# Outer-product recurrence and gated feed-forward on one core: another order of loads, v copies, units and split blocks

## The chip, the cores and the metric

The kernel runs on 1 core of one Trainium2 chip. The metric is the device time of one execution in microseconds (us), the median of 3 runs. Its engines are PE (matmuls, with PEld for the weight loads), DVE, ACT and POOL (elementwise work), and SP, which here only issues DMAs. POOL also issues the loads of the weights.

## What is computed

```python
f = 1.0 / (1.0 + np.exp(-f_logit))
for t in range(S):
    state = f[:, :, t, :, None] * state + np.einsum('bhd,bhe->bhde', k[:, :, t], v[:, :, t])
    y[:, :, t] = np.einsum('bhd,bhde->bhe', q[:, :, t], state)
...
x = np.ascontiguousarray(attn_out.transpose(0, 2, 1, 3)).reshape(B * S, H * D)
gate = np.maximum(x @ w_gate, 0.0)
val = x @ w_val
return (gate * val @ w_out).astype(np.float32)
```

There are 4 batches, 8 heads, 768 tokens and 48 columns a head, so x has 3072 rows of 384; the hidden width is 1536.

## The kernel before

**Units.** The recurrence is computed in chunks of 128 tokens. Two neighbouring chunks of a batch make a unit of 256 tokens; there are 12 units, in the order of batches 0 to 3 and then on along the sequence, so units 0 to 3 begin the four batches. A unit loads f, k, q and v (384 KB each, one DMA each, `load`, L465). ACT takes exp and log of f (L535, L542 or L537) to get the negative log of the decay. PE sums it along the chunk with triangular matrices (`cum`, L549 to L551). ACT takes the exponentials of the sums (L564 to L574). DVE and POOL multiply q and k by them; the products are called hats (L586 for units 0 to 3, L592 for the others). Units 0 to 3 turn the hats with PE (L624) and copy them out of PSUM (L401/402, the keys tq and tk of a unit); the later units turn them by a DMA on SP (L635). PE multiplies the turned hats to scores (L649), which are masked with `seen` (L663 on DVE, or L658 on ACT and L660 on POOL). The copies of v into a padded tile (`vpad`, four for a unit, keys v00 to v11) and, in units 0 to 3, of its rest (`vrest`, r0 and r1) are lines L399 (DVE), L401 (ACT) and L402 (POOL). PE builds from hats and v the new state (L704 or L714); DVE and POOL add it up and scale it (L510, L514, L517) with a decay that PE sums (L686, L690) and ACT exponentiates (L695), or, in units with the key td, that a small DMA fetches. PE forms the output of each chunk from masked scores, v and old state (L747, or L754 and L758), and a copy or a DMA brings it transposed into `xT`.

**Groups.** Two units make a group of 512 tokens for the feed-forward, so there are 6 groups. A group has 12 blocks of 128 hidden columns. For each block PE computes gate and value (L798, three matmuls of 512 columns each), ACT takes the relu of the gate (L803) and DVE the product into `gT` (L810). Then PE multiplies `gT` with `wo` (L828, 36 matmuls of 384 columns for every pair of chunks, in steps of three), ACT or DVE copies the result (L401/402) and SP stores it. `PARTS` says which blocks of a group are split: `(0, 2, 0, 3)` is chunks 0 and 1 of blocks 0 to 2, that is the first unit's half, with matmuls of 256 columns; before, only blocks 0 to 2 of group 0 are.

**Weights.** wg, wv and wo come in four slices of three blocks each, issued by POOL (L479), 12 DMAs. `FIRST` lists the first loads, and behind an @ which load a weight slice must wait for.

**Order.** Nothing is scheduled on the chip by rules: each operation has a number, and `SEQUENCE` lists for every engine, and for SP, the numbers in the order of issue. `HOMES` says which results follow each other in each of the 8 PSUM banks. `UNITS` names, for every unit, the engine of each movable step (the keys above, and x0, x1, o0, o1, q and k hats, masks m00 to m11, sum). Engines work strictly in the listed order and wait on semaphores for what they need. `FILLERS` puts warm-up matmuls on zeros (L879, 512 columns) ahead of the waits of some of the first PE steps: 38 in all. Operations that cross the two halves of the partitions on POOL wait for the one before.

The loads on SP begin f0, f1, q1, k0, k1, q0, v2, f2, v0, v1, k2, q2, f3, v3, k3, q3. On ACT the logs of units 0 and 1 come first. POOL has, among others, three copies of v0 and one of its rest, four of v1, one k hat of unit 0, three q hats, and between these the first weight issues. In the first 150 numbers unit 1 is ahead of unit 0 on PE, DVE and ACT for most steps: its hats are turned, its scores formed and its first output made sooner.

Of the kernel before, what the change touches and what calls it, by code (L numbers as in the profile page):

```python
# [5 lines left out]
AF = mybir.ActivationFunctionType  # L6
# [32 lines left out]
class Plan:  # L39
# [91 lines left out]
    def needs(self):  # L131
# [144 lines left out]
PARTS = {0: [(0, 2, 0, 3), (2, 4, 0, 3), (0, 4, 3, 12)]}  # L276
# [5 lines left out]
def bass_hgrn2_outer__then__ffn_reglu_kernel(  # L282
# [10 lines left out]
    B, H, S, D = q.shape  # L293
    C = 128
# [77 lines left out]
    def act_t(n):  # L372
        return dict(occ=0.8 if n == 768 else 0.06 + n / 1200.0, lat=0.16)
# [572 lines left out]
```

## Time and profile before

| | |
|---|---|
| median of 3 runs | 190.05 us (189.39 to 190.53) |
| the profiled execution | 190.12 us |
| its span, from first to last instruction | 188.9 us |
| granted TensorE clock, mean | 1.000 |
| POOL, busy | 103.1 us (55%) |
| DMA | 32.89 MB, mean 174 GB/s |

The profile shows one execution. In its timeline and chain the first number is the start, the second the length in us; "x3" is a count, and what stands in brackets is the idle time of the engine just before, and what ended it. In the groups by line the two numbers behind the bar are busy us in total and the mean ns of one. Matmuls overlap, so their lengths in the timeline are longer than the distance from one to the next; the chain shows the distances. A few matmul records are missing.

### The profile page before, as it was taken

To read this page: it belongs to the slowest core of one execution; us is meant where nothing else is said; L and a number is where in the kernel's file an instruction comes from. 1 tells how busy PE (TensorE), PEld (TensorE's weight loads), DVE (VectorE), ACT (ScalarE), POOL (GpSimd) and SP (SyncE) were. 2 spreads that over 40 slices of the span, in tenths; PEclk is the share of its full clock that TensorE was granted. 3 is DMA by queue.
4 is the path that set the end of the run, shared out by engine and by line. 5 is a ranking of instruction groups with operands and counts; after the bars stand their busy time and mean duration, and the time that the engine had idled before them with its cause. 6 is when DMAs were issued, how large, how long until landed. Compare 5 with 4: busy or idle time off the path is not lost.

```text
span 188.9 us, 4186 instructions
## 1 busy us (share of the span) xinstructions
PE 180.7 (96%) x1626; PEld 99.6 (53%) x1649; DVE 123.8 (66%) x227; ACT 120.5 (64%) x231; POOL 103.1 (55%) x138
## 2 busy tenths in 40 slices
PE   7899999999999999989999999999999999999995
PEld 2355584556654555534655445556555555444564
DVE  4169957778389898956687688996636653454320
ACT  3888869876789888966785776484284422334213
POOL 3299946998097795997744998732839100000000
PEclk9999999999999999999999999999999999999999
DMA  6999999998399999989999969878550240200025
GB/s 161 325 325 280 242 217 204 261 207 130 79 322 227 206 283 245 206 201 212 228 182 305 244 111 162 193 177 203 97 140 14 72 126 3 83 0 0 0 93 202
DMA packets 83167, 32.89 MB, mean 174 GB/s; under 512 B 75334, under 2 KB 83148, under 8 KB 83148
## 3 DMA queue, kind: packets, MB, share of 16 engines
q1 hardware_dynamic: 78348, 29.09, 65.3%
q0 software_dynamic: 4800, 3.54, 12.1%
q8 instruction: 13, 0.21, 0.4%
q14 instruction: 6, 0.05, 0.1%
HBM read 25.96 MB, written 4.73 MB: 162 GB/s over the span
## 4 chain that ended last, share of the span: by engine, by line
PE 82%; POOL 5%; DMA 4%; ACT 3%; issue 3%; DVE 2%; POOLq 0%
PE ps L798 48%; PE ps L828 23%; PE ps L649 3%; PE ps L747 2%; DMA f_in<-in_f_logit_dram 2%; DMA xT<-xn 2%; POOL vpad L402 2%; DVE gT L810 1%; PE ps L758 1%; PE ps L704 1%; POOL hats L586 1%; PE ps L624 1%; ACT bneg L542 1%; DVE hats L592 1%; POOL wg L479 1%
## 5 line engine op out<-in xcount | busy, mean ns | idle before, releaser
L810 DVE TENSOR_TENSOR gT<-relu,ps 128x512 bf16<-128x512 bf16 (+1 forms) x75 | 49.2, 682 | 22.5 <-PE ps L798 12.8
L803 ACT ACTIVATE relu<-ps 128x512 bf16<-128x512 f32 (+1 forms) x75 | 42.2, 579 | 31.3 <-PE ps L798 24.1
L798 PE MATMUL ps<-xT,wg 128*128 128x512 bf16 (+1 forms) x211 | 52.3, 370 | 1.4 <-issue 0.5
L798 PE MATMUL ps<-xT,wv 128*128 128x512 bf16 (+1 forms) x218 | 53.0, 370 | 0.6 <-issue 0.3
L828 PE MATMUL ps<-wo,gT 128*128 128x384 bf16 (+2 forms) x300 | 52.2, 320 | 0.0
L828 PEld LDWEIGHTS ps<-wo,gT 128*128 128x128 bf16 x300 | 28.1, 98 | 19.2
L592 POOL TENSOR_TENSOR hats<-q_in,expo 64x384 bf16<-64x384 f32 x28 | 27.8, 993 | 17.0 <-DMA q_in<-in_q_dram 9.8
L798 PEld LDWEIGHTS ps<-xT,wg 128*128 128x128 bf16 x225 | 21.0, 98 | 21.8 <-DMA xT<-xn 0.5
L798 PEld LDWEIGHTS ps<-xT,wv 128*128 128x128 bf16 x225 | 20.8, 98 | 20.8 <-ACT relu L803 0.3
L660 POOL TENSOR_TENSOR ptm<-ptm,seen 128x512 bf16<-128x512 bf16 x21 | 24.0, 1156 | 3.7 <-ACT ptm L658 3.5
L592 DVE TENSOR_TENSOR hats<-k_in,ps 64x384 bf16<-64x384 f32 x32 | 17.6, 551 | 4.5 <-ACT ps L574 4.0
L663 DVE TENSOR_TENSOR ptm<-ps,seen 128x512 bf16<-128x512 f32 x27 | 17.9, 683 | 2.9 <-PE ps L649 2.8
L517 POOL TENSOR_TENSOR st<-ssum,dec 128x384 bf16<-128x384 f32 x16 | 13.2, 828 | 5.3 <-DMA dec<-rates 3.5
L401 ACT ACTIVATE osb<-ps 128x384 f32<-128x384 f32 (+2 forms) x18 | 8.5, 470 | 10.6 <-PE ps L828 10.3
L658 ACT ACTIVATE ptm<-ps 128x512 bf16<-128x512 f32 x21 | 11.9, 597 | 5.2 <-PE ps L649 5.2
L567 ACT ACTIVATE expo<-ps 128x384 f32<-128x384 f32 x22 | 10.5, 487 | 6.9 <-DVE ps L556 6.2
L402 POOL CAST vpad<-v_in 64x384 bf16<-64x384 f32 x24 | 12.0, 501 | 1.3
L535 ACT ACTIVATE f_in<-f_in 128x768 f32<-128x768 f32 x12 | 10.1, 839 | 2.3 <-DMA f_in<-in_f_logit_dram 2.2
L514 DVE TENSOR_TENSOR ssum<-ps,st 128x384 f32<-128x384 f32 x16 | 8.8, 552 | 3.7 <-PE ps L704 3.1
L879 PE MATMUL ps<-zeros 128*128 128x512 bf16 x36 | 10.7, 434 | 0.2 <-issue 0.2
L574 ACT ACTIVATE ps<-ps 128x384 f32<-128x384 f32 x22 | 10.7, 490 | 0.0
L539 POOL TENSOR_TENSOR bneg<-f_in 128x384 bf16<-128x384 f32 x5 | 5.0, 1001 | 9.5 <-ACT f_in L537 9.5
(89 smaller groups left out, 175.4 us busy)
## 6 DMA issues: line engine op xcount, KB each, us to landing
f_in<-in_f_logit_dram SPq DMA_DIRECT2D x12, 384.0 KB, 5.6
q_in<-in_q_dram SPq DMA_DIRECT2D x12, 384.0 KB, 5.0
k_in<-in_k_dram SPq DMA_DIRECT2D x12, 384.0 KB, 4.8
v_in<-in_v_dram SPq DMA_DIRECT2D x12, 384.0 KB, 4.8
out_dram<-osb SPq DMA_DIRECT2D x22, 192.0 KB, 2.1
wg<-in_moe_w_gate_dram POOLq DMA_DIRECT2D x4, 288.0 KB, 7.8
wv<-in_moe_w_val_dram POOLq DMA_DIRECT2D x4, 288.0 KB, 7.9
wo<-in_moe_w_out_dram POOLq DMA_DIRECT2D x4, 288.0 KB, 8.2
```

Source lines behind the costliest of these rows:

```text
L402: return engine[e].tensor_copy(out, src)
L517: add(e, lambda: engine[e].tensor_tensor(t4(s_new), t4(tmp), rate, ALU.mult), [key] + dk, [f"S{b}_{y}"], **(dict(occ=0.79, lat=0.1) if e = ...
L574: add("ACT", lambda i=i, ex=ex: sc.activation(bc[i].ap[:, 0:HD] if in_place else ex[:, 1, :], bc[i].ap[:, 0:HD], AF.Exp, scale=1.0), [bc[i ...
L592: op = add(e, lambda i=i, n=n, x=x, e=e, y=y, lo=lo, exps=exps: engine[e].tensor_tensor(hats[64 * i:64 * i + 64, hi, y, x, :, 0:D], by_i[n ...
L658: add("ACT", lambda pt=pt, s=sj[j]: sc.activation(pt, s.ap[:, :].rearrange("p (n t) -> p n t", n=NP), AF.Copy), [sj[j]], [f"raw{mis[y]}_{j ...
L660: add("POOL", lambda pt=pt, mask=mask: gp.tensor_tensor(pt, pt, mask, ALU.mult), [f"raw{mis[y]}_{j}", "seen"], [f"raw{mis[y]}_{j}", f"ptm{ ...
L663: add("DVE", lambda pt=pt, mask=mask, s=sj[j]: ve.tensor_tensor(pt, s.ap[:, :].rearrange("p (n t) -> p n t", n=NP), mask, ALU.mult), [sj[j ...
L798: mm = te.matmul(bank.ap[:, 0:n], wt[:, kt, j * 128:(j + 1) * 128], xT[xi][:, kt, n0:n1], start=(kt == 0), stop=(kt == NK - 1))
L803: add("ACT", lambda: sc.activation(relu[ri][:, n0:n1], gate.ap[:, 0:n], AF.Relu), [gate], rk, **act_t(n))
L810: return ve.tensor_tensor(o, a, b, ALU.mult)
L828: mm = te.matmul(bank.ap[:, 0:cut[1] - cut[0]], gT[gi][:, j, r * C:(r + 1) * C], wo[:, j, cut[0]:cut[1]], start=(j == 0), stop=(j == NJ - 1))
L879: return te.matmul(bank[:, 0:WARM], zeros[:, 0:128], zeros[:, 0:WARM], start=True, stop=True, skip_group_check=True)
```

## The change

- SP: the loads begin v0, f0, f1, q0, k1, k0, q1, v1, f2, q2, k2, f3, v2, k3, q3, v3.
- ACT begins with three copies of v0 (v00, v11, v10, which were POOL's); the exponentials and logs of f come behind them, in the order exp f0, exp f1, log f0, log f1. Unit 0's other copies of v and its rest go to DVE (v01, r1) and POOL (r0). Of unit 1, v01, v00 and v11 are on ACT.
- Unit 0 is ahead of unit 1 in hats, scores, masks and state. On POOL the first hats are unit 0's q0, then unit 1's q1 and q0; unit 0's k hats are both on DVE.
- POOL issues wg0 behind unit 1's q1 hat, wg1 behind its q0 hat, wv0 when q2 has landed, wv1 two copies later, wg2 to wg3 behind unit 1's state, wv3 behind a mask of unit 2, and wo0 to wo2 behind unit 3's copies of v3, wo3 behind one more mask.
- Ahead of the feed-forward's first matmul PE has the same steps as before, but for unit 2's decay sum and unit 1's second output, which stand behind it.
- Blocks 0 to 5 of groups 0 and 1 are computed in halves. In group 1 some of the first unit's halves stand ahead of the first L828 of group 0.
- The 38 warm-up matmuls become 30, 18 of them ahead of the first cumulative sum.
- `SEQUENCE`, `HOMES` and the engines in `UNITS` are others for all units. The sum of the two halves of the logs is POOL's in units 3 to 11; before, DVE had it in units 4, 9, 10 and 11. In unit 6, POOL makes the unit's four q hats one after the other; before, one of unit 7 stood ahead of the fourth. The load of q for unit 6 is the fourth behind unit 5's transposes on SP; it was the fifth.
- `load` can take half the heads, and `unit` can take exp and log in two parts (key fs); no unit sets it and no load is halved.

```diff
-FILLERS = {67: (9, 0), 106: (4, 0), 83: (6, 1), 121: (3, 1), 125: (4, 3), 90: (7, 2), 134: (4, 1), 138: (1, 0)}
+FILLERS = {67: (18, 0), 85: (3, 0), 83: (1, 4), 90: (1, 6), 123: (2, 6), 87: (2, 0), 125: (3, 0)}
...
     "ACT": [
-        65, 66, 103, 69, 104, 73, 107, 108, 74, 111, 112, 70, 84, 10, 230, 231, 130, 116, 246, 81, 117, 94, 133, 136, 245, 234, 235, 238, 239,
+        77, 82, 80, 65, 103, 66, 104, 70, 69, 74, 133, 73, 107, 111, 112, 116, 94, 115, 108, 10, 242, 243, 122, 120, 100, 130, 97, 246, 247, 136,
...
     "SP": [
-        37, 41, 43, 38, 42, 39, 48, 45, 40, 44, 46, 47, 49, 52, 50, 51, 142, 271, 143, 311, 144, 274, 145, 272, 273, 317, 388, 389, 320, 435,
+        40, 37, 41, 39, 42, 38, 43, 44, 45, 47, 46, 49, 48, 50, 51, 52, 283, 142, 143, 323, 145, 144, 284, 285, 286, 329, 424, 425, 445, 471,
...
-FIRST = 'f0 k0 q0 v0 f1 k1 q1 v1 f2 k2 q2 v2 f3 k3 q3 v3 wg0@v2 wv0@f0 wg1@v2 wv1 wg2@v2 wv2@f3 wg3@q2 wv3@f0 wo0@f0 wo1@f3 wo2 wo3@f3'
-PARTS = {0: [(0, 2, 0, 3), (2, 4, 0, 3), (0, 4, 3, 12)]}
+FIRST = 'f0 k0 q0 v0 f1 k1 q1 v1 f2 k2 q2 v2 f3 k3 q3 v3 wg0@q0 wv0@q2 wg1 wv1 wg2@v0 wv2 wg3@k0 wv3@q1 wo0@v1 wo1@q0 wo2@k1 wo3'
+PARTS = {0: [(0, 2, 0, 6), (2, 4, 0, 6), (0, 4, 6, 12)], 1: [(0, 2, 0, 6), (2, 4, 0, 6), (0, 4, 6, 12)]}
```

The numbers of the first steps are the same in both kernels: 65 and 66 are exp and log of f0, 103 and 104 of f1; 77, 80 and 82 the copies v00, v10 and v11 of unit 0; 116 the copy v01 of unit 1; 94 and 133 the decays of units 0 and 1; 108 unit 1's k exponential; 37 to 52 the loads f0, k0, q0, v0, f1 and so on. From about 230 on the numbers are shifted, as the split blocks add operations.

More of the change, by code (lines that the diff above doesn't have):

```diff
@@ L534, in unit @@
         on.update(UNITS.get(u, {}))
-        add("ACT", lambda: sc.activation(raw["f"], raw["f"], AF.Exp, scale=-1.0), [f"f{li}"], [f"f{li}"], **act_t(2 * HD))
-        if on["sum"]:
+        fs = on.get("fs")
+        if fs:
+            for x in range(2):
+                part, hs = raw["f"][:, x * HD:(x + 1) * HD], slice(x * NP, (x + 1) * NP)
+                add("ACT", lambda part=part: sc.activation(part, part, AF.Exp, scale=-1.0), [f"f{li}x{x}", f"f{li}"], [f"f{li}x{x}"], **act_t(HD))
+                add("ACT", lambda hs=hs: sc.activation(bn[:, :, hs, 0:D], by_i["f"][:, :, hs, :], AF.Ln, bias=1.0),
+                    [f"f{li}x{x}", f"f{li}", f"bneg{bi}"], [f"bn{bi}x{x}"], **act_t(HD))
+        else:
+            add("ACT", lambda: sc.activation(raw["f"], raw["f"], AF.Exp, scale=-1.0), [f"f{li}"], [f"f{li}"], **act_t(2 * HD))
+        if fs:
+            pass
+        elif on["sum"]:
             add("ACT", lambda: sc.activation(raw["f"], raw["f"], AF.Ln, bias=1.0), [f"f{li}"], [f"f{li}"], **act_t(2 * HD))
@@ L543, in unit @@
                 [f"bn{bi}"], **act_t(2 * HD))
-        bkeys = [f"bneg{bi}", f"bn{bi}"]
+        bkeys = [f"bneg{bi}", f"bn{bi}"] + ([f"bn{bi}x{x}" for x in range(2)] if fs else [])
         bc = [Bank("bc"), Bank("bc")]
```

67 lines of the change are left out of this document (33 added, 34 removed), and 83 rows, old and new, of tables (SEQUENCE, UNITS).

## Prediction

> **What bounds the kernel now.** I read the page's first two parts, then the chain that ended last, then the timeline of the first 27 us with the waits inside it.
>
> ```profile
> PE 180.7 (96%) x1626; PEld 99.6 (53%) x1649; DVE 123.8 (66%) x227; ACT 120.5 (64%) x231; POOL 103.1 (55%) x138
> PE   7899999999999999989999999999999999999995
> PEclk9999999999999999999999999999999999999999
> ```
>
> TensorE is busy in every slice at full clock, so from the first feed-forward matmul on, its own work sets the end. Before that it is held up by one chain:
>
> ```profile
> 15.41 0.52 POOL vpad L402
> ...
> 22.67 0.51 PE ps L747 x28
> 23.29 0.20 PE ps L690 x8
> 23.48 0.35 PE ps L798 x3
> ...
> 25.38 0.66 PE ps L798 x6
> ...
> 33.48 3.99 PE ps L798 x18
> ```
>
> The chain goes through the load of f, the logarithms and the hats, and from 15.41 on through copies of v on POOL, with weight issues among them, until the outputs (L747) at 22.67 that the feed-forward (L798) needs. It opens at 23.48. What lies ahead of it is waiting filled with warm-up matmuls (L879), so an earlier opening moves the end one for one, less what is moved behind it and new waits. Behind it TensorE's pauses are short but for one, which has a part of its own below.
>
> **The change: the opening.** Loads, by the first instructions that waited for them:
>
> ```profile
> 7.95 0.56 DVE L586 TENSOR_TENSOR hats<-k_in,expo 128x384 bf16<-128x384 f32 x1 [4.14 <-DMA k_in<-in_k_dram]
> 14.00 0.55 DVE L399 TENSOR_REDUCE vpad<-v_in 64x384 bf16<-64x384 f32 x1 [0.57 <-DMA v_in<-in_v_dram]
> ```
>
> These are the fourth and the ninth load: one lands every (14.00 - 7.95)/5 = 1.21 us, the n-th at 7.95 + 1.21(n - 4), the first at 4.3. The new order on SP is v0, f0, f1, q0, k1, k0, q1, v1, f2, q2: v0 lands at 4.3, f0 at 5.5 (it was first), f1 6.75, k0 10.4, q1 11.6, v1 12.8 (it was tenth), q2 15.2.
>
> ```profile
> 5.21 0.84 ACT L542 ACTIVATE bneg<-f_in 128x768 bf16<-128x768 f32 x1
> 5.96 0.83 ACT L535 ACTIVATE f_in<-f_in 128x768 f32<-128x768 f32 x1
> 6.10 0.34 PE L550 MATMUL ps<-bneg,upto 128*128 128x384 bf16 x1 [0.69 <-ACT bneg L542]
> 6.69 0.47 ACT L574 ACTIVATE expo<-ps 128x384 f32<-128x384 f32 x1
> 15.75 1.47 ACT L401 ACTIVATE vrest<-v_in 64x384 bf16<-64x384 f32 x3
> 16.60 3.12 DVE L663 TENSOR_TENSOR ptm<-ps,seen 128x512 bf16<-128x512 f32 x5
> 18.12 0.60 ACT L401 ACTIVATE xT<-ps 128x384 bf16<-128x384 f32 x1 [0.17 <-PE ps L747]
> 75.18 6.37 POOL L592 TENSOR_TENSOR hats<-q_in,expo 64x384 bf16<-64x384 f32 x6 [2.18 <-DMA q_in<-in_q_dram]
> DMA to landing us min/median/max: 6.5/7.8/10.6
> ```
>
> Queued ACT steps follow each other by 0.47 (v copies), 0.75 (768 wide) and 0.39 us (384 wide); DVE masks by (3.12 - 0.69)/4 = 0.61; a POOL hat takes 6.37/6 = 1.06. The last line is from the view of wg, its four slices' time from issue to landing. By hand along each queue of the changed kernel:
> - ACT: three copies of v0 from 4.3, exp of f0 at 5.75, exp of f1 at its landing 6.75, log of f0 7.50 to 8.34, log of f1 8.25 to 9.09. The first cumulative sum is thus at 8.4 against 6.10: **2.3 us late**. Exponentials run from 8.98 to 12.0.
> - ACT then stands before v1's copy until v1 lands at 12.8; queued behind are unit 0's decay (13.3), another copy, and unit 1's k exponential (13.9 to 14.4). DVE waits for both: state 13.5, sum, unit 1's last k hat 14.55, first mask at 15.0.
> - DVE runs eight steps without a break (masks and one transpose copy): 15.0 + 7 x 0.61 + 0.69 = 20.0. The last mask feeds unit 1's first output; with its 16 matmuls (0.3 us by row 22.67) and one cumulative sum (row 6.10) the feed-forward opens at **20.6**. Its inputs are there before: xT of unit 0 at about 19.9; wg0, issued on POOL at 12.6 behind a q hat that starts when q1 lands at 11.6, at 19.1 by the shortest landing.
>
> So the late logs cost nothing in the end: v0's copies no longer stand on POOL from 15.41, and v1's are done by 18.7 on ACT and POOL. In the timeline, before:
>
> ```profile
> 23.34 0.49 PE L798 MATMUL ps<-xT,wg 128*128 128x256 bf16 x3
> ```
>
> Against 23.34 (the chain's 23.48 leaves out what overlaps the matmuls before) this is **-2.7**.
>
> What goes behind the opening: unit 2's decay sum (row 23.29, 0.20 us) and unit 1's second output (row 22.67; its 28 matmuls issue in 0.4): **+0.6**. New waits there: that output waits for a PSUM bank that ACT empties at 21.2, which is 0.2 us, and unit 1's first half block waits for an xT copy that ACT starts behind unit 2's exponentials at 22.4 and that takes 0.60, 0.4 us more: **+0.6** (0 to 1.2).
>
> **Halves.** Nine more blocks are split. TensorE: six 256-wide matmuls take 0.66 (row 25.38), that is 0.110 each; eighteen 512-wide 3.99, 0.222 each. Two halves cost a whole, so 0.
>
> ```profile
> L803 ACT ACTIVATE relu<-ps 128x512 bf16<-128x512 f32 x69 | 40.0, 596 | 30.1 <-PE ps L798 23.0 <-DVE gT L810 5.2 <-PE ps L690 1.1
> L803 ACT ACTIVATE relu<-ps 128x256 bf16<-128x256 f32 x6 | 2.2, 383 | 1.2 <-PE ps L798 1.0
> L810 DVE TENSOR_TENSOR gT<-relu,ps 128x512 bf16<-128x512 bf16 x69 | 47.1, 705 | 21.0 <-PE ps L798 11.3 <-ACT relu L803 8.6
> L810 DVE TENSOR_TENSOR gT<-relu,ps 128x256 bf16<-128x256 bf16 x6 | 2.2, 417 | 1.5 <-PE ps L798 1.5
> ```
>
> ACT pays 9 x (2 x 383 - 596) = 1.5 us, DVE 9 x (2 x 417 - 705) = 1.2 us. Both wait for the matmuls at these lines (23.0 and 11.3 us), which covers it; without that cover the end would pay up to 1.5. I take 0.
>
> **Weights.** Two are doubtful: wg2, which POOL issues at 22.8 behind unit 1's state, and wo0, which it issues behind a copy of v3, now the sixteenth load.
>
> ```profile
> 14.00 1.15 SPq L465 DMA_DIRECT2D f_in<-in_f_logit_dram  x1
> DMA to landing us min/median/max: 9.0/9.0/9.0
> 19.89 2.99 SPq L465 DMA_DIRECT2D q_in<-in_q_dram  x1
> DMA to landing us min/median/max: 15.3/15.3/15.3
> 33.77 1.54 POOL L479 DMA_DIRECT2D wo<-in_moe_w_out_dram  x2
> DMA to landing us min/median/max: 5.5/8.2/9.1
> 42.65 1.14 PE L828 MATMUL ps<-wo,gT 128*128 128x384 bf16 x6
> L660 POOL TENSOR_TENSOR ptm<-ptm,seen 128x512 bf16<-128x512 bf16 x21 | 24.0, 1156 | 3.7 <-ACT ptm L658 3.5
> ```
>
> The landings are those of load f3, of the last load q3 and of the four wo slices. wg2 lands at 29.3 (shortest) to 30.6 (median); TensorE asks for it 24 half steps of 0.33 after the opening, with the waits above at 29.2. Fewer weights are open in the queue then than before, so I hold it near the short end.
> The sixteenth load landed at 19.89 + 15.3 = 35.2. Then POOL has two copies (0.5 each) and a mask (1.16): wo0 is issued at 37.4 instead of 33.77 and lands at 42.9 to 46.5. Before, TensorE took 42.65 - 23.34 = 19.3 us from the opening to its first L828. Now 0.6 is moved behind, 0.6 is waited, and put ahead of it are seven half steps of group 1 (7 x 0.33) and scores, outputs and a state of units 2 and 3 (68 matmuls at row 22.67's 0.51/28, 1.3 us): it asks at 20.6 + 19.3 + 0.6 + 0.6 + 2.3 + 1.3 = 44.7. With a landing between the shortest and the median, 45.1, it waits 0.4 (0 to 1.8). The two don't add up, since a TensorE held up by wg2 asks later for wo0: **+0.4** for both (0 to 1.8).
>
> **The pause at 84.**
>
> ```profile
> 80.50 2.13 SPq L635 DMA_TRANSPOSE qkT<-hats  x1
> 85.16 0.62 PE L649 MATMUL ps<-qkT 48*128 48x128 bf16 x16 [1.06 <-issue]
> ```
>
> Unit 6's scores wait for its second transpose, issued at 80.50 when the fifth of the POOL hats of row 75.18 ends; POOL itself had waited 2.18 for q. The new POOL order does unit 6's four hats first (one hat, 1.06 us, sooner), and SP loads that q fourth instead of fifth behind unit 5's transposes (1 us or more). The scores stand 0.4 us of TensorE work nearer to their cumulative sum. 2.0 - 0.4 exceeds 1.06: the pause goes, **-1.0** (-1.06 to +1).
>
> All other orders behind 50 us are new too, and the trace of before can't show their waits. The list of waits gives TensorE's own few; I take the same again, bounded by the size of the one pause in row 85.16 either way (-1.06 to +1.06).
>
> **Sum**, from the profiled execution's 190.12 (span 188.9 and 1.2 around it; the median is 190.05): -2.7 + 0.6 + 0.6 + 0 + 0.4 - 1.0 = -2.1, so **188.0**.
>
> **Rivals.**
> - The pause at 84 stays or comes back in another stage: 189.1. For it: every margin behind 50 us is laid out anew. Against: the two steps that made it are ahead of where they were.
> - Slower, by late weights: under weight traffic the loads f3 to q3 landed at 23.0 and 35.2, three intervals of 4.1 us instead of 1.21. wg0, wg1, wv0 and wv1 are now all issued by 17.3, with six loads still open at 15.2. At 4.1 each v3 lands at 39.8, wo0 is issued at 42.0 and lands 8.2 later at 50.2; TensorE waits 5.5 instead of 0.4: 193.1. It decides from v3's landing: past about 37 the gain is gone. Against it: the DMA engines must carry the same bytes by then, which gave 35.2. The Trainium skill (DMA: Bandwidth & Descriptors, Queues, rings and completion order) says that a DMA engine takes turns between queues a packet at a time, so queues of unlike packets need not share evenly; the 4.1 agrees. By that rule alone the time would be this rival's 193.1, by the conserved bytes the forecast's.
> - The clock. Eight warm-up matmuls fewer, and TensorE pauses 1.1 us ahead of the first cumulative sum, longer than the 0.69 at 6.10.
>
> ```profile
> 1.66 3.76 PE L879 MATMUL ps<-zeros 128*128 128x512 bf16 x9
> ```
>
>   A 512-wide matmul took 0.42 there, before the clock opened, against the 0.222 of row 33.48. Another 3.8 us at half speed ahead of the opening would cost up to 1.9: 189.9. The Trainium skill (TensorE: Matmul & The Clock Gate, Part 1) puts the fall back at an idle window of some 3.4 us; by that rule nothing happens here, and no run here shows the limit.
> - The opening doesn't come sooner: if v1 lands no sooner than as the tenth load, at 15.2, ACT, DVE and the opening shift by 2.4 to 23.0; with the moved work and waits, and without the weights' 0.4, that gives 190.0.
> - No new waits at the opening, wo0 in time and some of the short pauses behind it gone: 186.5.
>
> **Chances.** Forecast (186.9 to 189.0) 0.57; pause stays 0.15; late weights 0.11; clock 0.05; no earlier opening 0.06; better 0.06. The range leaves out the worst of the late weights and the last of the better: 186.4 to 190.7. A measurement can tell 0.5% (0.95 us) of 190.05 from no change; below 189.1 is faster: 0.57 + 0.06 = 0.63; slower (over 191.0) is the late weights: 0.11; within: 0.26.
>
> **What would show it.** Right: first cumulative sum at about 8.4 and feed-forward at about 20.6; masks back to back on DVE from 15.0; first L828 matmul near 45 with at most half a us of wait for wo; no pause of a us at unit 6's scores. Wrong: ACT stands for v1 past 13.5; v3 landing after 37; granted clock under 1 between 7 and 20 us; several pauses of half a us behind 50 us.

## The result, and the profile after

The changed kernel takes **190.5 us** (median of 20 executions, 189.84 to 192.18) against 189.91 for the kernel before, run beside it (20, 188.72 to 192.31): a ratio of **1.0049**, 95% interval 1.0027 to 1.007. Ratios, here and below, compare means and leave out slow executions (here two of the kernel before), so they are not the quotients of the medians. That is about 0.9 us slower, where 2.1 us faster had been forecast.

The kernel was profiled twice: the execution shown first took 191.24 us (span 190.0), the one of the run after_again 189.78 (span 188.6). The kernel before was profiled a second time too (before_again, 189.36, span 188.1). The first profile after, its first two parts:

```profile
PE 181.9 (96%) x1695; PEld 104.3 (55%) x1695; DVE 123.2 (65%) x234; ACT 121.2 (64%) x246; POOL 102.6 (54%) x134
PE   7988999999999979999998999999999999999995
PEclk9999999999999999999999999999999999999999
```

The clock is full throughout. What stands out behind the opening is the 7 in the fifteenth slice, near 70 us; it was a 9. The chain that ended last, of the same profile:

```profile
8.49 5.34 DMA v_in<-in_v_dram
16.22 1.21 DVE ptm L677 x2
...
23.01 0.77 POOL st L521
23.78 7.14 DMA wg<-in_moe_w_gate_dram
31.05 2.44 PE ps L812 x18
...
64.86 4.81 DMA qkT<-hats
69.92 0.62 PE ps L663 x16
```

Before, this chain was the loads and POOL's copies of v up to the opening at 23.48, and TensorE from there. Now it runs on past the opening, over POOL's state of unit 1 (L521) and the DMA of wg2 to 31.05, and once more over a transposing DMA of unit 5 to 69.92. TensorE's longest waits behind the opening in after_again, the last three columns being us in total, times and the longest:

```profile
PE ps L812 <- DMA wg<-in_moe_w_gate_dram: 1.1, 1, 1.1
PE ps L663 <- DMA qkT<-hats: 1.0, 1, 1.0
```

The timeline of after_again at the places that the prediction named:

```profile
8.27 0.34 PE L564 MATMUL ps<-bneg,upto 128*128 128x384 bf16 x1 [1.14 <-ACT bneg L556]
12.71 0.52 ACT L403 ACTIVATE vpad<-v_in 64x384 bf16<-64x384 f32 x1 [1.02 <-DMA v_in<-in_v_dram]
14.99 1.28 DVE L677 TENSOR_TENSOR ptm<-ps,seen 128x512 bf16<-128x512 f32 x2
16.79 3.19 DVE L677 TENSOR_TENSOR ptm<-ps,seen 128x512 bf16<-128x512 f32 x5
20.70 0.49 PE L812 MATMUL ps<-xT,wg 128*128 128x256 bf16 x3
30.61 0.59 PE L812 MATMUL ps<-xT,wg 128*128 128x512 bf16 x2 [1.09 <-DMA wg<-in_moe_w_gate_dram]
46.44 0.65 PE L842 MATMUL ps<-wo,gT 128*128 128x384 bf16 x3
64.17 0.50 PE L812 MATMUL ps<-xT,wv 128*128 128x256 bf16 x3 [0.31 <-DVE ssum L518]
69.25 0.62 PE L663 MATMUL ps<-qkT 48*128 48x128 bf16 x16 [0.99 <-DMA qkT<-hats]
```

The first five rows are the opening: first cumulative sum 8.27, v1 in at 12.7, masks without a break from 14.99, feed-forward at 20.70. It comes about as forecast (8.4, 12.8, 15.0, 20.6). Of the others, all but the first L842 show where the gain is given back. In the second profile of the kernel before:

```profile
23.70 0.49 PE L798 MATMUL ps<-xT,wg 128*128 128x256 bf16 x3
...
84.64 0.62 PE L649 MATMUL ps<-qkT 48*128 48x128 bf16 x16 [0.18 <-issue]
```

So the opening is 3.0 us sooner, profile against profile. But the pause at unit 6's scores, 1.06 in the profile that the prediction rested on, is 0.18 here: of the two profiles of that kernel, one has it.

The same, stage by stage. Columns: window, its length, then busy us and count of PE, PEld, DVE, ACT and POOL, granted clock, DMA share, GB/s. First before_again, then after_again:

```profile
24.00:46.00 22.00, 21.84 (x202) 13.12 (x204) 15.75 (x30) 17.34 (x35) 17.91 (x23) 1.00 1.22 214
...
60.00:76.00 16.00, 15.63 (x206) 8.67 (x208) 14.39 (x26) 13.40 (x27) 12.17 (x14) 1.00 1.07 257
```

```profile
24.00:46.00 22.00, 20.58 (x255) 13.93 (x255) 17.76 (x36) 17.54 (x39) 14.75 (x20) 1.00 1.08 204
...
60.00:76.00 16.00, 14.43 (x221) 8.78 (x222) 12.78 (x26) 12.13 (x24) 12.85 (x15) 1.00 1.08 254
```

TensorE's idle time grows by 1.26 us in the first of these stages and by 1.20 in the second.

The whole difference of these two profiles, from distances between matmuls (each against the same step in the other profile): opening -3.1 by the weight loads, waits behind it +2.2 (3.26 against 1.06: wg2 1.04, unit 5's scores 1.06, the block at 64 us 0.38, an xT copy 0.21, less 0.25 at unit 6's scores and 0.2 in small ones), work moved behind the opening +0.6, a wait for a PSUM bank in it +0.33, the halves +0.16. That makes +0.2. TensorE's last matmul starts at 185.96 in before_again and at 186.39 in after_again, 0.43 later, so 0.2 us is not placed.

**Theories** with which the experiments began. A: the opening is worth its 3 us, and single waits behind it, at wg2, at unit 5's scores and at unit 7's xT (103 us, 0.73 us in the first profile), give it back; mend each and its us comes back. B: something behind the opening sets a floor, so a wait that is mended comes back at another place. Ratios below are to the kernel before on the same chip, with 95% intervals; 0.005 is 0.95 us.

### The profile page after: what moved, and what is told of

Its sections match the earlier page's. It is cut to its first block, busy times and chain, and to the rows that moved or that the text cites. A ratio compares the mean times of both kernels' runs of the same rounds, so it can differ in the third digit from the quotient of the medians.

```text
span 190.0 us, 4338 instructions
## 1 busy us (share of the span) xinstructions
PE 181.9 (96%) x1695; PEld 104.3 (55%) x1695; DVE 123.2 (65%) x234; ACT 121.2 (64%) x246; POOL 102.6 (54%) x134
## 3 DMA queue, kind: packets, MB, share of 16 engines
q0 software_dynamic: 4800, 3.54, 12.8%
## 4 chain that ended last, share of the span: by engine, by line
PE 77%; DMA 9%; SPq 4%; POOL 3%; ACT 2%; DVE 2%; issue 1%; POOLq 0%; DVEq 0%
PE ps L812 43%; PE ps L842 24%; SPq L469 4%; DMA wg<-in_moe_w_gate_dram 4%; DMA v_in<-in_v_dram 3%; PE ps L663 3%; DMA qkT<-hats 3%; POOL hats L606 2%; PE ps L761 2%; PE ps L772 1%; PE ps L768 1%; POOL st L521 1%; PE ps L563 1%; PE ps L718 1%; DVE ptm L677 1%
## 5 line engine op out<-in xcount | busy, mean ns | idle before, releaser
L824 DVE TENSOR_TENSOR gT<-relu,ps 128x512 bf16<-128x512 bf16 (+1 forms) x84 | 50.2, 626 | 38.8 <-PE ps L812 34.0
L812 PE MATMUL ps<-xT,wg 128*128 128x512 bf16 (+1 forms) x252 | 56.1, 349 | 1.2 <-DVE gT L824 0.7
L812 PE MATMUL ps<-xT,wv 128*128 128x512 bf16 (+1 forms) x252 | 55.9, 349 | 0.2 <-DVE ssum L518 0.2
L842 PE MATMUL ps<-wo,gT 128*128 128x384 bf16 (+2 forms) x300 | 52.4, 320 | 0.0
L842 PEld LDWEIGHTS ps<-wo,gT 128*128 128x128 bf16 x300 | 28.4, 98 | 19.3
L812 PEld LDWEIGHTS ps<-xT,wg 128*128 128x128 bf16 x252 | 23.6, 98 | 20.8 <-DMA xT<-xn 1.2
L812 PEld LDWEIGHTS ps<-xT,wv 128*128 128x128 bf16 x252 | 23.4, 98 | 19.9 <-DVE ssum L518 0.4
L521 POOL TENSOR_TENSOR st<-ssum,dec 128x384 bf16<-128x384 f32 x16 | 13.2, 830 | 6.9 <-DVE ssum L518 5.8
L403 ACT ACTIVATE osb<-ps 128x384 f32<-128x384 f32 x18 | 8.8, 491 | 11.6 <-PE ps L842 11.1
L403 ACT ACTIVATE vpad<-v_in 64x384 bf16<-64x384 f32 x20 | 10.4, 519 | 4.9 <-DMA v_in<-in_v_dram 4.7
L553 POOL TENSOR_TENSOR bneg<-f_in 128x384 bf16<-128x384 f32 x9 | 9.0, 998 | 6.4 <-ACT f_in L551 6.3
L663 PE MATMUL ps<-qkT 48*128 48x128 bf16 x192 | 8.0, 217 | 2.3 <-ACT dec L709 1.1
L404 POOL CAST vpad<-v_in 64x384 bf16<-64x384 f32 x17 | 8.5, 501 | 3.0 <-DMA v_in<-in_v_dram 2.2
```

What stands on the lines that cost most here:

```text
L403: return sc.activation(out, src, AF.Copy)
L521: add(e, lambda: engine[e].tensor_tensor(t4(s_new), t4(tmp), rate, ALU.mult), [key] + dk, [f"S{b}_{y}"], **(dict(occ=0.79, lat=0.1) if e = ...
L663: mm = te.matmul(sj[j].ap[:, p * C:(p + 1) * C], tokens(u, y, 1, p, lo, lo + D), tokens(u, y, 0, p, lo, lo + D))
L812: mm = te.matmul(bank.ap[:, 0:n], wt[:, kt, j * 128:(j + 1) * 128], xT[xi][:, kt, n0:n1], start=(kt == 0), stop=(kt == NK - 1))
L824: return ve.tensor_tensor(o, a, b, ALU.mult)
L842: mm = te.matmul(bank.ap[:, 0:cut[1] - cut[0]], gT[gi][:, j, r * C:(r + 1) * C], wo[:, j, cut[0]:cut[1]], start=(j == 0), stop=(j == NJ - 1))
```

## The experiments

**Single waits.** Of each edit the lists in `SEQUENCE` are shown, cut to the place. In f_behind unit 7's load of f (445) goes behind unit 5's transposes (471, 470):

```diff
 "SP":
-  424, 425, 445, 471, 470, 612,
+  424, 425, 471, 470, 445, 612,
```

> The changed kernel, but on SP the load of f that stands ahead of unit 5's two transposes (issued at 61.94 in the profile after) is put behind them. Theory (each pause of TensorE behind the opening is a misplaced step of its own, and what is taken away comes off the end): the transposes are issued about 0.5 us sooner and have less traffic ahead of them, the 1.1 us pause at unit 5's scores goes or shrinks to under 0.3, and the median falls from 190.5 to 189.4 to 189.7. Rival (the supply from POOL, ACT and the DMAs sets a floor between 55 and 105 us): the pause goes, but waits of about the same size come up within the next 20 us, and the median stays at 190.3 to 190.7.

Measured: 194.64 us, 1.0293 (1.0251 to 1.0334). Timeline of f_behind, ACT and TensorE, then its windows:

```profile
69.59 0.84 ACT L548 ACTIVATE f_in<-f_in 128x768 f32<-128x768 f32 x1 [4.83 <-DMA f_in<-in_f_logit_dram]
71.50 0.62 PE L664 MATMUL ps<-qkT 48*128 48x128 bf16 x16 [3.24 <-issue]
```

```profile
72.00:74.00 2.00, 1.29 (x57) 1.02 (x56) 2.00 (x5) 2.00 (x5) 1.93 (x3) 0.85 0.88 213
74.00:76.00 2.00, 2.00 (x21) 0.70 (x10) 0.38 (x1) 1.04 (x3) 1.60 (x2) 0.50 1.14 330
```

The transpose did land sooner, at 66.1, 3.3 us after its issue instead of 5.2. But the load of f, now issued at 64.25, landed at 69.56, and ACT stood 4.83 us before f with relus queued behind it. TensorE paused 3.24 us, until the first of these relus was done (70.81 to 71.40 on ACT). A shorter pause of 0.54 us followed at 72.87. The granted clock fell to 0.50 at about 73.4, which added to the loss. Neither theory had this. The Trainium skill (TensorE: Matmul & The Clock Gate, What's actually happening) puts the fall of the clock behind an idle window of some 3.4 us, free-running; here the longest pause ahead of the fall was 3.24 us.

In xt_first the second transpose of unit 7's output (660) goes ahead of a store (239) and of the decays' DMA of unit 8 (769):

```diff
 "SP":
-  227, 655, 239, 769, 660, 665,
+  227, 655, 660, 239, 769, 665,
```

> The changed kernel, but on SP the transpose of unit 7's second xT goes ahead of one store and one small DMA of unit 8's rates (issued at 99.16 instead of 100.11). Theory (separate pauses): the 0.9 us pause of the feed-forward at 103.4 falls to under 0.2 and the median from 190.5 to about 189.7. Rival (a floor of supply): the pause returns in the next blocks and the median stays at 190.3 to 190.7.

Measured: 190.07 us, 1.0036 (1.0014 to 1.0058). There is no wait at 103 us in it, but in after_again, without the edit, there is none either (0.1 us), at the same ratio. So that wait of the first profile came and went by execution, and the edit was worth nothing that can be measured.

In wg2_early POOL issues wg2 (57) ahead of unit 1's last mask (131), and wv2 and wg3 (58, 59) ahead of unit 1's state (141):

```diff
 "POOL":
-  118, 56, 117, 131, 35, 141, 57, 58, 59, 289,
+  118, 56, 117, 57, 131, 35, 58, 59, 141, 289,
```

> The changed kernel, but POOL issues wg2 ahead of unit 1's last mask and wv2 and wg3 ahead of unit 1's state (wg2 at about 19.7 instead of 23.78). Theory (wg2's place in POOL's order makes the 0.56 us wait at 31.0): wg2 lands by 30.4, the wait falls under 0.15, and the median falls to about 190.0. Rival 1 (the weights' own queue lands a slice every 2.2 to 2.9 us however early it is issued): wg2 lands at 30.3 to 30.9, the wait falls by less than 0.4. Rival 2 (floor): the wait goes and the pause at unit 5's scores grows from 1.1 to 1.6; median 190.5.

Measured: 189.34 us, 0.9987 (0.9962 to 1.0013), against 1.0036 (1.0019 to 1.0052) for the changed kernel as it is: 0.9 us back. TensorE's three longest waits in wg2_early; wg is neither among them nor among the shorter ones (the first and the third lie ahead of the opening):

```profile
PE ps L449 <- DVE zeros L392: 1.3, 1, 1.3
PE ps L664 <- DMA qkT<-hats: 1.1, 1, 1.1
PE ps L565 <- ACT bneg L557: 0.5, 1, 0.5
```

Issue and landing of wg2, by line and window, in after_again and then in wg2_early:

```profile
22.65 0.80 POOL L483 DMA_DIRECT2D wg<-in_moe_w_gate_dram  x1
...
DMA to landing us min/median/max: 7.6/7.6/7.6
```

```profile
18.59 0.78 POOL L484 DMA_DIRECT2D wg<-in_moe_w_gate_dram  x1
...
DMA to landing us min/median/max: 10.6/10.6/10.6
```

The issue is 4.06 us sooner, the landing 1.1 (29.1 against 30.3): the slice stands behind those issued before it, which land at 17.8, 22.0, 24.1 and 27.1 in both. The Trainium skill (DMA: Bandwidth & Descriptors, Two DMAs through the same engine are not ordered) says that what stands in one queue of a DMA engine starts in order; the landings agree. In before_again wg2 landed at 30.7. **The opening moved 3 us, the weights 0.4**, and that is the wait. Theory A holds here, by the times. Between the two profiles the stretch from the opening to TensorE's last matmul shrinks by 0.5 us only (165.69 to 165.20), so in that execution part of the wait came back elsewhere.

**The opening by itself.** opening_alone is the kernel before with the new order up to the opening on all engines (loads, ACT's v copies first, unit 0 ahead, weights as changed), v2 the twelfth load, and the old order behind it:

```diff
-FILLERS = {67: (9, 0), 106: (4, 0), 83: (6, 1), 121: (3, 1), 125: (4, 3), 90: (7, 2), 134: (4, 1), 138: (1, 0)}
+FILLERS = {67: (18, 0), 85: (3, 0), 83: (1, 4), 90: (1, 6), 123: (2, 6), 87: (2, 0), 125: (3, 0)}
 "SP":
-  37, 41, 43, 38, 42, 39, 48, 45, 40,
+  40, 37, 41, 39, 42, 38, 43, 44, 45,
 "ACT":
-  65, 66, 103, 69, 104, 73,
+  77, 82, 80, 65, 103, 66, 104, 70,
```

> The kernel before with the opening of the changed one alone: loads (v2 the twelfth, ahead of f3), v copies, engines and orders of units 0 and 1 and the warm-ups up to the first feed-forward matmul are those of the changed kernel; all later steps, banks and the three half blocks are those of before (three ACT copies of v2 stand a few steps later, since v2 lands later). Unit 1's second output and unit 2's decay sum stand ahead of the opening, as before. Theory (the opening gains about 1.6 us by itself, of which the two moved steps take 0.6 and a bank wait 0.3): feed-forward opens at about 22.6 against 23.3, and the median is 189.1 to 189.4 against 189.9. Rival (the gain of the opening is lost again behind it, because the weights wg2 and wo0 and the loads k2, v2, v3 come no sooner): opening at 22.6, but waits of 0.7 or more between 24 and 46 us, and a median of 189.9 or more.

Measured: 194.4 us, 1.0205 (1.0146 to 1.0263). TensorE's timeline and windows in it:

```profile
22.31 0.35 PE L732 MATMUL ps<-qkT,st 128*32 128x128 bf16 x12 [1.47 <-DVE hats L571]
23.93 0.20 PE L671 MATMUL ps<-away,other 128*128 128x16 bf16 x1 [0.87 <-DVE hats L571]
```

```profile
22.00:22.50 0.50, 0.19 (x15) 0.19 (x18) 0.50 (x2) 0.06 (x1) 0.50 (x2) 1.00 1.24 202
22.60:23.00 0.40, 0.40 (x23) 0.19 (x9) 0.40 (x2) 0.00 (x0) 0.40 (x1) 0.50 1.26 202
23.00:29.00 6.00, 5.13 (x44) 4.19 (x41) 2.25 (x5) 1.82 (x5) 1.03 (x3) 0.50 1.25 206
```

Unit 1's second output and unit 2's decay sum, which this kernel keeps ahead of the feed-forward, wait 1.47 and 0.87 us (for banks that DVE's hats still use, by the rows), and the opening is at 24.2 instead of the expected 22.6. The clock falls to half between the two waits, at about 22.6, and stays there past 29. So it does not say what the opening is worth. It shows 2.3 us of waits at two steps that the change puts behind the opening; the kernel before has them ahead too and opens at 23.7. The two of six executions at full clock still took 191.7 and 192.6; the profiled one is not among them.

**The same kernel again, and f.** The changed kernel, unedited (after_again), and the kernel before, unedited (before_again), for what belongs to a kernel and what to an execution:

> The changed kernel, unaltered, for a second profile. Theory: the loads land without the two gaps of 1.7 us of the first profile (v1 at 12.6 to 12.9), feed-forward opens at 20.5 to 21.2, TensorE waits about 1.0 us for wg2 and about 1.1 at unit 5's scores, and the pause at 103 is under 0.3; median 0.3 to 0.7% over that of before. Rival (the gaps in the loads belong to this order of loads): v1 lands at 13.5 or later again and the opening is at 21.6 or later.

> The kernel before, unaltered, for a second profile. If its pause of 1.1 us at unit 6's scores belongs to every execution, it is there again at 84 to 85. If it was this one execution's (which at 190.12 was 0.2 to 0.7 over the medians of before), the pause is under 0.4 here, and the span is under 188.3; then the forecast's minus 1.0 had nothing to take away.

Measured: 189.97 us, 1.0036 (1.0019 to 1.0052), and 189.42 us, 1.0004 (0.9988 to 1.0021). In the first profile after, two of the loads up to v1 came 1.7 us apart instead of 1.2, and v1 only at 13.83:

```profile
13.85 0.52 ACT L403 ACTIVATE vpad<-v_in 64x384 bf16<-64x384 f32 x1 [2.00 <-DMA v_in<-in_v_dram]
21.85 0.49 PE L812 MATMUL ps<-xT,wg 128*128 128x256 bf16 x3
31.05 0.81 PE L812 MATMUL ps<-xT,wg 128*128 128x512 bf16 x3 [0.40 <-DMA wg<-in_moe_w_gate_dram]
```

The opening is 1.15 us later here than in after_again, but behind wg2's wait only 0.4 is left of it. So most of a us at the opening is lost again while wg2 lands no sooner. Unit 5's pause is there in both (chain row 69.92 of the one, timeline row 69.25 of the other).

f_between puts f between the two transposes, and its exponential (616) two steps later on ACT, behind a copy of scores and a relu; wg2_and_f has this and the edit of wg2_early:

```diff
 "SP":
-  424, 425, 445, 471, 470, 612,
+  424, 425, 471, 445, 470, 612,
 "ACT":
-  390, 432, 616, 430, 386, 617,
+  390, 432, 430, 386, 616, 617,
```

> The changed kernel, but the load of f stands on SP between unit 5's two transposes instead of ahead of both, and on ACT its exponential stands behind two more steps (a copy of unit 4's scores and a relu), so that ACT doesn't stand for it. Theory (the 1.1 us pause at unit 5's scores is made by this load's place): the second transpose lands at 67.5 to 68.5 instead of 69.67, the pause falls under 0.3, and the median falls by about 1.0 us against the changed kernel. Rival (floor of supply): as much is waited within the next 20 us, no change. Second rival: f's exponential comes later, ACT stands for it as in the run before this one, and the pause is as long as it was or longer.

> Both edits together: wg2, wv2 and wg3 issued earlier on POOL, and the load of f between unit 5's transposes with its exponential later on ACT. Theory (the pauses are separate): the two gains add, about 1.9 us off the changed kernel, a median 0.4 to 0.7% under that of before. Rival (floor): no faster than the wg2 edit alone, which was level with before.

Measured: 190.66 us, 1.0084 (1.006 to 1.0109), and 190.16, 1.0028 (1.0007 to 1.0049). TensorE at unit 5's scores in f_between:

```profile
69.84 0.62 PE L664 MATMUL ps<-qkT 48*128 48x128 bf16 x16 [1.37 <-DMA qkT<-hats]
```

The pause grew: the second transpose, which still has the load of f ahead of it, and now directly, landed no sooner (69.6). So this edit doesn't tell whether the load holds it up. In f_behind, with the load behind both, each transpose took 3.3 us. That wg2's edit again takes off 1.1 us (1.0084 to 1.0028) confirms that part a second time.

**The logs.** In logs_first v0 is the third load, the exponentials and logs come first in ACT's order, and seven of the first 18 warm-up matmuls go:

```diff
 "SP":
-  40, 37, 41, 39,
+  37, 41, 40, 39,
 "ACT":
-  77, 82, 80, 65, 103, 66, 104, 70, 69, 74, 133, 73, 107, 111, 112, 116,
+  65, 103, 66, 104, 70, 69, 74, 133, 73, 107, 111, 112, 77, 82, 80, 116,
```

> The changed kernel, but with f0 and f1 as first and second load and v0 third, the exponentials and logs first on ACT, the three copies of v0 in ACT's idle time ahead of v1, and 11 warm-ups instead of 18 ahead of the first cumulative sum. Theory of the prediction (v1's landing sets the opening, the late logs cost nothing): first cumulative sum 1.0 to 1.6 sooner, v1 lands and feed-forward opens at the same time within 0.3 us, median unchanged within 0.3. Rival (the late logs hold up the hats, and with them the opening): opening 0.5 to 1.5 sooner. Neither theory sees it slower unless ACT's copies of v0 hold up unit 0's state.

Measured: 191.72 us, 1.009 (1.0056 to 1.0123). The first log on ACT, and three of the waits of TensorE in its profile:

```profile
7.52 1.58 ACT L557 ACTIVATE bneg<-f_in 128x768 bf16<-128x768 f32 x2 [1.20 <-DVE halves L392]
PE ps L813 <- DMA xT<-xn: 0.8, 1, 0.8
PE ps L729 <- ACT vpad L404: 0.8, 1, 0.8
PE ps L813 <- DMA wg<-in_moe_w_gate_dram: 0.5, 1, 0.5
```

The logs did not come sooner: by the profile, ACT's first log waited 1.20 us for a step on DVE (L392, which fills constants), and it began at 7.52, where it began at 7.39 in after_again; the first cumulative sum is at 8.42, against 8.27. So **the run did not make the logs early and cannot say what late logs cost.** The first feed-forward matmul is at 21.66, a us later than in after_again, with v1 in at 12.7 in both. The 0.8 for ACT's v copies (L404), which now stand behind the exponentials, is the opening's delay, but for 0.2. Unit 5's pause is gone (its transposes landed at 67.5, still with the load of f ahead of them), but others came at 88 to 103 us. In seven of its eight executions the mean granted clock was 0.98 or 0.99, so part of the ratio is the clock's.

**What holds up the transpose.** In the records of single packets, wherever unit 5's last transpose (in f_behind and its like the load of f) landed late, it did so 2.0 to 2.8 us behind the start of a 16 KB packet of the queue that carries instructions, of which the page of the first profile after counts, with their bytes:

```profile
q8 instruction: 13, 0.21, 0.5%
```

The packet at 66 to 67 us, while unit 5's transposes were in flight, started at 67.2 in the first profile after and at 66.9 in after_again; the transpose landed at 69.7 and 69.0. In logs_first it started at 70.2, behind the landing, and in before_again at 71.6, behind it too. If this is the cause, more or fewer instructions ahead should shift the packet and with it the pause. On top of wg2_early, shift16 has 4 warm-ups of 512 columns replaced by 20 of 16 columns, shift6 has 2 replaced by 8, and shift_m4 has 4 left out:

```diff
-FILLERS = {67: (18, 0), 85: (3, 0), 83: (1, 4), 90: (1, 6), 123: (2, 6), 87: (2, 0), 125: (3, 0)}
+NARROW = {67: 20}
+FILLERS = {67: (14, 0), 85: (3, 0), 83: (1, 4), 90: (1, 6), 123: (2, 6), 87: (2, 0), 125: (3, 0)}
...
+                    for _ in range(NARROW.get(op.idx, 0)):
+                        te.matmul(banks[k][:, 0:16], zeros[:, 0:128], zeros[:, 0:16], start=True, stop=True, skip_group_check=True)
```

> The kernel with wg2 issued earlier; four of the eighteen 512-wide warm-ups ahead of the first cumulative sum are replaced by twenty 16-wide ones, so that TensorE's stream of instructions has 16 matmuls more in about the same time, and nothing else moves. Theory (a 16 KB packet of the instruction queue q8, which comes by TensorE's count of instructions, arrives while unit 5's second transpose is in flight; in seven runs the transpose landed 2.1 to 2.5 us after that packet's start, and in the one run where the packet came after the landing there was no pause): the packet comes about 3 us sooner, at 62.5 to 64, the transpose lands by 67.5, the pause at unit 5's scores falls from 1.17 to under 0.2, and the median falls by about 1.0 us against the wg2 edit alone, to 0.4 to 0.7% under before. Rival (the transpose is late through the loads ahead of and behind it on SP): it lands at 68.3 to 68.7 as before, the pause stays 1.0 to 1.2, level with before.

> As the run before this one, with two wide warm-ups replaced by eight narrow ones: 6 matmuls more. Theory (instruction packet): it comes at 64.5 to 65.5 instead of 66.4, the transpose lands 2.1 to 2.5 later, at 66.8 to 67.8, and the pause is under 0.3. Rival: landing at 68.3 to 68.7, pause 1.0 to 1.2.

> The kernel with wg2 issued earlier and 14 instead of 18 warm-ups ahead of the first cumulative sum: 4 matmuls fewer, and TensorE idle 2 us there instead of 0.5. Theory (instruction packet): it comes at 67 to 68 instead of 66.4; if the transpose is still in flight then it lands at 69.2 to 70.3 and the pause grows to about 2; if the packet comes after its landing the pause goes. Rival: landing at 68.3 to 68.7 and a pause of 1.0 to 1.2. The clock stays at 1.0 in both.

| run | us | ratio | packet starts | transpose lands | pause at unit 5 | at 103 us |
|---|---|---|---|---|---|---|
| wg2_early | 189.34 | 0.9987 (0.9962 to 1.0013) | 66.4 | 68.5 | 1.17 | none |
| shift16 | 191.23 | 1.0081 (1.0052 to 1.0111) | 64.8 | 66.9, 67.6 | 0.43 | 2.17 |
| shift6 | 190.81 | 1.0111 (1.0072 to 1.0151) | 66.0 | 68.1 | 0.99 | 1.09 |
| shift_m4 | 189.19 | 0.9975 (0.9951 to 1.0000) | 65.9 | 68.0 | 0.78 | 1.01 |

The pauses here are by distances between matmuls. In shift16 the first of the two transposes landed 2.1 us behind the packet, the second 2.8. The landing follows the packet, but the packet did not go where it was expected: 16 instructions more, 6 more and 4 fewer all moved it sooner, by 1.6, 0.4 and 0.5 us.

The other suspect is the load of f, which the change put ahead of unit 5's transposes; in the kernel before, a load of v stood there and f behind. With f ahead and the packet in flight, the last transpose took 4.7 to 6.0 us (nine profiles). With f ahead and the packet at another time it took 3.8 (logs_first) and 4.0 (whole_blocks); with f behind, and landed ahead of the packet, 3.2 to 3.4 (f_behind and the three runs below that have f there); in before_again 3.2. So by these runs the load accounts for some 0.8 us at most, and the rest goes with the packet. **What holds up the transpose stays open** all the same: this is a correlation over thirteen profiles, and no run moved the packet as intended. And in shift16, where unit 5's pause shrinks, one of 2 us stands at the xT transpose of 103 us. That speaks for theory B.

**All three mended.** f_behind_acts has f behind the transposes as in f_behind, and ACT's exponential and log of it (616, 617) later, behind the relus that TensorE waited for; three_mended adds the edits of wg2_early and xt_first:

```diff
 "SP":
-  424, 425, 445, 471, 470, 612,
+  424, 425, 471, 470, 445, 612,
 "ACT":
-  432, 616, 430, 386, 617, 568, 402, 394, 477, 438,
+  432, 430, 386, 568, 402, 394, 616, 477, 617, 438,
```

> The changed kernel with the load of f behind both of unit 5's transposes on SP (as in f_behind) and, on ACT, that f's exponential and log four and three steps later, behind the relus that TensorE waited for there. Theory (the pause at unit 5's scores is the second transpose, which is in flight when the instruction packet comes at 66 to 67.5): the transpose lands at 65.5 to 66.5, ahead of the packet, f lands at 68.5 to 70 without ACT standing for it, the pause is under 0.2, and the median falls about 1.0 us against the changed kernel, to 0.996 to 1.000 of before. Rival (floor of supply between 55 and 105): other waits of together 1 us come up by 105, ratio 1.003 to 1.006. The packet hypothesis alone would be wrong if the transpose is issued at 62.9 or sooner and still lands after 68.

> Three edits together: wg2, wv2 and wg3 issued earlier on POOL (wg2_early), f behind unit 5's transposes with its ACT steps later (f_behind_acts), and unit 7's xT transpose ahead of a store and a small DMA on SP (xt_first). Theory (separate pauses, each worth its own length): no wait for wg2 at 30, none at unit 5's scores, none at 102; opening at 20.5 to 21.2, waits behind it 1.0 to 1.5 us in all as in before, median 0.7 to 1.2% under before (187.1 to 188.1 where before is 189.4). Rival (floor): level with before, 0.997 to 1.002.

Measured: 191.81 us, 1.0124 (1.0083 to 1.0165), and 189.86, 1.0032 (1.0008 to 1.0056). In f_behind_acts unit 6's cumulative sum waits 0.86 us in one piece for a copy of xT on ACT. The same row in three_mended:

```profile
71.67 0.34 PE L564 MATMUL ps<-bneg,upto 128*128 128x384 bf16 x1 [1.17 <-ACT xT L404]
```

In three_mended the waits at wg2, at unit 5's scores and at 103 us are all gone, with the opening at 20.75. But f landed at 69.0 instead of 65.5, ACT's work on it ran into the copies of xT, and unit 6's cumulative sum waited 1.5 us in two pieces. three_mended_2 puts 616 and 617 further back, behind the first and the second of unit 4's two copies to xT:

```diff
 "ACT" (against three_mended):
-  402, 394, 616, 477, 617, 438, 398, 442,
+  402, 394, 477, 438, 616, 398, 442, 617,
```

> As three_mended, but f's exponential and log stand two steps further back on ACT, behind unit 4's two xT copies, for the first of which TensorE waited 1.5 us at 71.7 in three_mended while ACT stood for f (which landed at 69.05). Theory (the delay of what was in flight at 67 is handed from the transpose to f and ends there, if nobody needs f): no wait over 0.4 between 60 and 100, waits behind the opening 1.5 to 2.0 us in all, median 0.5 to 1.0% under before. Rival (floor: the delay is handed on to unit 7's cumulative sum, which needs that f, or to its hats): a wait of about 1 us between 73 and 90, ratio 1.000 to 1.004.

Measured: 189.44 us, 1.0018 (0.9991 to 1.0046). TensorE in three_mended_2:

```profile
81.80 0.82 PE L813 MATMUL ps<-xT,wv 128*128 128x512 bf16 x3 [1.04 <-ACT relu L818]
...
89.24 0.62 PE L664 MATMUL ps<-qkT 48*128 48x128 bf16 x16 [0.36 <-DMA qkT<-hats]
```

Now the us stands at 81.8. From the opening to TensorE's last matmul it takes 165.60 us, against 165.69 in after_again: with all three waits mended, the waits are the same in sum. From some 55 us on the runs speak for theory B: the units' chain of f, hats and transposes over SP, ACT and POOL is just in time, and what was mended at one place was late at the next. That no order is free of such waits is not shown.

**The halves.** whole_blocks is the changed kernel with the nine new split blocks whole, each at the place of its later half, their banks shared out anew:

```diff
-PARTS = {0: [(0, 2, 0, 6), (2, 4, 0, 6), (0, 4, 6, 12)], 1: [(0, 2, 0, 6), (2, 4, 0, 6), (0, 4, 6, 12)]}
+PARTS = {0: [(0, 2, 0, 3), (2, 4, 0, 3), (0, 4, 3, 12)]}
```

> The changed kernel with the nine more split blocks (3 to 5 of group 0, 0 to 5 of group 1) whole again, each at the place of its later half; all other steps stand in the same order, and the numbers of SEQUENCE and HOMES are laid out to match. Theory of the forecast (halves cost nothing): the same waits for wg2 and at unit 5's scores, median within 0.4 us of the changed kernel. Second theory (the first unit's halves are what TensorE has to do while unit 1's xT copies, unit 2's transposes and scores are awaited): waits of together 0.5 to 2 us more between 21 and 46, slower by as much. Rival (the halves' 1.5 us on ACT and 1.2 us on DVE delay the recurrence): faster by 0.5 to 1.5.

Measured: 191.74 us, 1.013 (1.0087 to 1.0173), 1.8 us more than with the halves. The longest of TensorE's waits in it from 23 to 49 us:

```profile
28.89 0.40 PE L646 MATMUL ps<-qkT 48*128 48x128 bf16 x8 [0.49 <-ACT relu L800]
30.80 0.59 PE L795 MATMUL ps<-xT,wg 128*128 128x512 bf16 x2 [0.87 <-DMA wg<-in_moe_w_gate_dram]
...
46.01 0.21 PE L711 MATMUL ps<-vpad,hats 64*128 64x96 bf16 x1 [0.67 <-ACT ptm L655]
46.99 0.66 PE L825 MATMUL ps<-wo,gT 128*128 128x384 bf16 x3 [0.47 <-DVE ptm L660]
```

With two of 0.36 at 23.2 and 48.7 they make 3.2 us; in after_again the same stretch has 1.4 (xT 0.21, wg2 1.04, unit 3's state 0.18). The halves cost next to nothing, and are what TensorE does where it would otherwise wait.

No kernel of these is clearly faster than the one before. The best, shift_m4, touches 1.0000 with the end of its interval.

## Why the prediction was wrong, point by point

Two steps failed: the waits behind 50 us, which the forecast put at nothing new (they came to 1.4), and the pause at 84, whose 1.0 was hardly there to gain. A third, the weights, was too small by 0.6.

- **The opening, -2.7: right.** 20.70 against a forecast 20.6, by the path forecast. It is -3.0 between the second profiles (23.70 before) and -1.5 between the first ones (21.85 against 23.34); in wg2_early, f_between and three_mended the opening lies at 20.7 to 20.8. The rival "no earlier opening" is out. In the first profile after, v1 was a us late by gaps in the loads; ACT stood for it until 13.85, past the 13.5 that the prediction gave as a sign of being wrong.
- **Late logs cost nothing: as far as the trace shows.** In after_again ACT had stood 1.02 us when v1 came, so the exponentials behind the late logs were not what it waited for. logs_first was to test this and did not.
- **Moved work +0.6 and two new waits there, +0.6: right in sum.** The waits were 0.33 for the bank (forecast 0.2) and 0.21 for the xT copy (forecast 0.4), together 0.54.
- **Halves 0: right in cost** (+0.16 on TensorE: a half's three matmuls take 0.328 in the timeline's distances, the whole 0.647), but the step that it prices is not the one that matters: undone, they cost 1.8.
- **Weights +0.4: too small.** It was wg2 alone, and 1.04. POOL's issue at 22.65 and TensorE's asking at 29.5 were as forecast (22.8, 29.2). The choice that failed is "I hold it near the short end": the slice took 7.6, not 6.5. wo0 came in time, but that it landed at 44.3, near the forecast 45.1, is luck: it was issued at 39.9 instead of 37.4 and took 4.4 us instead of 7.7. The first L842 is at 46.4 instead of 44.7; 1.04 of this is the wait for wg2. The rival of late weights at v3 and wo0 did not come: v3 landed at 37.9 and at 35.2 in the two profiles, and no wo was waited for in either, so its "past about 37 the gain is gone" was wrong too.
- **The pause at 84, -1.0: a failed step.** The pause is gone, as forecast; but in another execution of the kernel before there was 0.18 by its row (0.25 by distances) to take away. The forecast's base of 190.12 was the execution that had it. Whether the two steps that were named for it take it away can't be seen where it is hardly there.
- **"I take the same again" for the orders behind 50 us: the other failed step, and the larger.** Unit 5's scores now wait 1.0 to 1.1 us in both profiles after, and the block at 64 us 0.3 to 0.4 for DVE's sum behind POOL's four hats in a row: 1.4 where the sum had nothing. The transpose that unit 5's scores wait for took 5.2 us; it took 3.2 in before_again, where the load of f stood behind it. The rival "the pause comes back in another stage" named this; its bound of 1.06 was about its size. What it did not have is that the pause had hardly been there before, so that it was a loss of 1.1 and not the return of a gain.
- **The clock rival: out** for this change; the granted clock is 1.000 in both profiles.

Put together, by the second profiles: -3.1 for the opening, +0.6 and +0.54 for what was moved and its waits, +0.16 for halves, +1.04 for wg2, +1.44 for unit 5 and the block at 64, -0.25 at unit 6, -0.2 in small waits, and +0.2 not placed: +0.4, where the medians of the two repeats differ by 0.55 us. The forecast's -2.1 is 2.5 away from it: 1.4 by the waits behind 50 us, 0.75 by the pause at 84, 0.64 by wg2, 0.16 by the halves, less 0.4 by the opening; the rest is below 0.1.

Shown by experiment: wg2's wait, twice, at 0.9 and 1.1 us; the halves; that the pauses behind 55 us, mended, were followed by others. Only read from traces: that unit 5's and unit 6's pauses trade places through the new order, and that late logs are harmless. Open: why the transpose takes 5.2 us with the new order.

## What to carry to other kernels

A pause of a us in one profile may belong to that one execution; its removal is credited only when a second profile has it too. A sooner opening is worth what the next fixed arrival leaves of it: here 3 us sooner met a stream of weights that came 0.4 us sooner, so what the new stage needs must be pulled forward with it. Where a chain behind it is just in time, mending one wait there can show at the next; the count to watch is the sum of the waits, not the one that was mended. And an edit that is to make a step early has done so only if the trace shows it early: the logs of logs_first stood first in the order and came no sooner.

## What the runs showed of the hardware

- The granted clock fell to 0.50 at about 73.4, 1.9 us after the end of a TensorE pause of 3.24 us and with one of 0.54 us between (f_behind), and at about 22.6, 0.3 us after the end of a pause of 1.47 us (opening_alone). A pause of 2.00 us that ended at 103.7 left it at 1.00 (shift16), as did pauses of 1.0 to 1.2 us in after_again and three_mended. So in these runs the length of the longest pause alone did not decide it.
- A weight slice issued 4.06 us sooner landed 1.1 us sooner (wg2_early against after_again); under load its landing followed the slices ahead of it more than its issue.
- The last transposing DMA of unit 5 took 3.3 us from issue to landing in f_behind and 5.2 in after_again; how much of this is the load ahead of it and how much the packet of instructions, which starts 2.0 to 2.8 us before such late landings, was not separated by a run.
- Of two executions of one kernel, one had loads 1.7 us apart where the other had 1.2, and the opening was 1.15 us later.
